# Layer norm of three blocks: the columns of x loaded and normalised on GpSimd, in place of rows normalised and transposed on TensorE

## The chip, the cores and the metric

The kernel runs on one core of one Trainium2 chip. The core has five engines, each with a queue of its own that it works through strictly in order: TensorE (PE in the profile; its weight loads are listed apart as PEld), VectorE (DVE), ScalarE (ACT), GpSimd (POOL) and SyncE (SP, which here only issues DMAs). They wait for each other through semaphores. The metric is the device time of one launch in microseconds (us).

## The reference

One transformer block for S = 2048 tokens of D = 448 values, with 16 heads of 28 and an MLP of 1792 columns, all in float32. A vector `c` gives the scale and shift of both layer norms and the gates:

```python
mod = (silu(c) @ w_mod).reshape(1, 6, 1, 448)
sa, ca, ga, sb, cb, gb = mod[:, 0], ..., mod[:, 5]
h = layernorm(x) * (1 + ca) + sa
x = x + ga * (softmax_attention(h @ wqkv) @ wo)
h = layernorm(x) * (1 + cb) + sb
x = x + gb * (gelu(h @ w1 + b1) @ w2 + b2)
```

The layer norm takes mean and deviation of each token over its 448 values. The change concerns the first layer norm alone, and of it the part for tokens 512 to 2047.

## The kernel before

**Tiling.** The tokens are cut into four blocks of 512 (`NB`), the 448 values into four chunks of 128 (`NC`; the last has 64 values and holds them twice, for a high and a low part). A matmul contracts over the partitions, so the first layer norm's result h has to lie by columns: a chunk is a tile [128 values, 512 tokens]. x lies by rows, [128 tokens, 448 values], four such row tiles to a block. Weights and activations of the dense layers are split into a high part (rounded to the matmul's input type) and a low part (what is left), and a product is three sums of products. Such a product of 448 values takes 11 matmuls (`mm_acc`, L406).

**Stages.** Up to 25 us the kernel loads, computes the modulation and lays block 0 out by columns. Then comes phase 1 (25 to 165 us): the projections to q, k and v, block after block. Phase 2 (165 to 789 us) is the attention in 256 steps, phase 3 (up to the end) the MLP.

**Phase 1.** A loop over the blocks b makes a list of tasks; n counts them. For block 0 they are seven tasks of q and k (n = 0 to 6), four of v (n = 7 to 10), and the first q and k tasks of block 1 (n = 11 and 12); for blocks 1 and 2, five of q and k (n = 0 to 4), four of v (5 to 8), and the next block's first two (9 and 10). A task is 11 matmuls into a PSUM buffer "pa", of which there are two; on PE four or five matmuls for the row maxima of the scores follow it (`emit_task`, L486). DVE reduces each of these (L491); for some, two key chunks are taken in one pass, after a relu by ACT (L499). What maxima are left over when phase 1 ends are done in phase 2, up to three to a step, until step 234.

After a q or k task ACT copies the sum out of PSUM ("full", three buffers, L442), ACT or DVE makes the high part (L445), POOL the low part (L449), and SP stores both (L452); SP also copies the rows that lie over into another place (L388). After a v task ACT copies out of PSUM (L468), which frees the buffer for the next task but one.

**The first layer norm of blocks 1 to 3** is spread over the tasks of the block before. `ln1_stages` has eight stages. Stages 0 to 3 take mean and variance of a row tile (DVE, L209 and L210); the last of them makes variance plus eps (DVE, L214), its power -0.5 (POOL, L216), and minus the mean times that (DVE, then POOL, L277). Stages 4 to 7 write a normalised row tile "xn" (ACT, two instructions, L242 and L243). Then `h_chunk(b + 1, xs, k)` runs at k = n - 6 in block 0 and n - 4 after that: four transposes on PE put a chunk of the four row tiles into one PSUM buffer (L286, called from `transposes`), ACT scales and shifts it by the modulation's columns (L307), ACT makes the high part (L291), POOL the low part (L293, for the last chunk L295). A chunk's transposes stand on PE behind the maxima of task n; its three other instructions stand behind the task's own work on ACT and POOL.

In a task with a `h_chunk`, and in the first four of block 1, `p1_n[1]` is false: the sixth of the PSUM buffers for maxima ("o") is needed for the transposes there, so one maximum fewer can stand beside a pair.

**What sets the order.** Every engine's instructions stand in the order in which this loop emits them. Nothing reorders them on the chip.

Of the kernel before, what the change touches and what calls it, by code (L numbers as in the profile page):

```python
# [13 lines left out]
F32 = mybir.dt.float32  # L14
# [32 lines left out]
def tile_adaln_block(ctx: ExitStack, tc: tile.TileContext, x, wqkv, wo, w1, b1, w2, b2, c, w_mod, out):  # L47
# [90 lines left out]
    for tag, shape, n in (  # L138
        ("mv", [128, 4, 2], 2), ("nm", [128, 4], 1), ("st", [128, 6], 2), ("ve", [128, 4], 2), ("rs", [128, 4], 2),
    ):  # L140
        sbt(tag, shape, bufs=n)
    m32s = [sbt(f"m32_{i}", [128, 32], F32R) for i in range(2)]
    d0 = slot4("d0", [512], F32)
# [120 lines left out]

    def ln1_stages(b):
        mv = []
        mr = []

        def stat(t):
# [3 lines left out]
            if t == 3:  # L273
                nm = sbt("nm", [128, 4])
                dve.tensor_scalar(out=nm, in0=mv[0][:, :, 0], scalar1=-1.0, scalar2=None, op0=ALU.mult)
                rs = ln_rstd(mv[0], 4)
                pool.tensor_tensor(out=nm, in0=nm, in1=rs[0][2], op=ALU.mult)  # L277
                mr.extend([rs[0][2], nm])

        return [lambda xs, t=t: stat(t) for t in range(4)] + [  # L280
            lambda xs, t=t: xs.append(ln1_apply_act(b, t, *mr)) for t in range(4)
        ]
# [16 lines left out]
    def h_chunk(b, xs, k, p=None):  # L299
# [3 lines left out]
        if p is None:  # L303
            p = ps_o()
            transposes(p, xs, k)
# [48 lines left out]
    v_sb = [sb.tile([128, 4, H, 32], F32, tag=f"slot_v{i}", name=f"v{i}", bufs=1) for i in range(4)]  # L354

    def v_init(i):
        pool.memset(v_sb[i][:, :, :, DH : DH + 1], 1.0)
        pool.memset(v_sb[i][:, :, :, DH + 1 : 32], 0.0)
# [164 lines left out]
    for m32 in m32s:  # L523
        pool.memset(f(m32)[:, 16:32], 0.0)

# [280 lines left out]
    for k in range(NC):  # L806
        lo0.append(h_chunk(0, xs0, k, p0[k]))
# [24 lines left out]
    stages = ln1_stages(1)  # L832
    for b in range(NB):
# [8 lines left out]
        if more:  # L842
            stages, later = stages[-4:] if b else stages, ln1_stages(b + 2) if b + 2 < NB else None
            xs_next = []
            tasks += [(b + 1, 0, 0), (b + 1, 1, 0)]
        for n, (tb, kind, g) in enumerate(tasks):
# [10 lines left out]
            p1_n[1] = not (more and (0 <= k < NC)) and not (b == 1 and n < 4)  # L857
# [18 lines left out]
            if more:  # L876
                k = n - (6, 4, 4, 4)[b]

                if b == 0 and n in (0, 1, 3, 4):
                    x = 2 * n if n < 2 else 2 * n - 2  # L880
                    for fn in stages[x : x + 2]:
                        fn(xs_next)
                if b and n < 4:
                    stages[n](xs_next)
# [664 lines left out]
```

## Time and profile before

| | us |
|---|---|
| median of three runs (lowest to highest) | 1091.16 (1090.96 to 1091.35) |
| the profiled execution's own time | 1092.34 |
| its span, from first to last instruction | 1090.6 |
| phase 1, in the span | 25 to 165 |
| PE busy in the span | 1081.5 |
| DVE, ACT, POOL busy in the span | 800.8, 696.7, 231.5 |

The profiled execution took 1.2 us longer than the median, and 1.7 us of it lie outside the span. Stretches are given by the span's clock. A row of the timeline gives the start, the duration of the row in us, the engine, the line of the kernel, the operation, what it writes and reads by the program's names, the shapes, and a count if several alike were joined. A bracket at the end tells how long the engine had been idle, and what it had waited for. SPq rows are DMA issues: the duration is that of the issue on SP, not of the transfer.

### The profile page before, as it was taken

To read this page: it belongs to the slowest core of one execution; us is meant where nothing else is said; L and a number is where in the kernel's file an instruction comes from. 1 tells how busy PE (TensorE), PEld (TensorE's weight loads), DVE (VectorE), ACT (ScalarE), POOL (GpSimd) and SP (SyncE) were. 2 spreads that over 40 slices of the span, in tenths; PEclk is the share of its full clock that TensorE was granted. 3 is DMA by queue.
4 is the path that set the end of the run, shared out by engine and by line. 5 is a ranking of instruction groups with operands and counts; after the bars stand their busy time and mean duration, and the time that the engine had idled before them with its cause. 6 is when DMAs were issued, how large, how long until landed. Compare 5 with 4: busy or idle time off the path is not lost.

```text
span 1090.6 us, 20665 instructions
## 1 busy us (share of the span) xinstructions
PE 1081.5 (99%) x8231; PEld 659.3 (60%) x8231; DVE 800.8 (73%) x1369; ACT 696.7 (64%) x883; POOL 231.5 (21%) x215
## 2 busy tenths in 40 slices
PE   8999999999999999999999999999999999999998
PEld 6766775444444444444444444545488888888887
DVE  6979788999999989988888988584755565464322
ACT  4655657888888888888888888687943321211111
POOL 1543330011011011024231410216114032061000
PEclk9999999999999999999999999999999999999999
DMA  9342262122121201143322423111343301002000
GB/s 304 141 154 74 89 206 86 44 67 57 50 76 61 77 28 58 56 121 86 103 68 78 130 64 95 58 31 60 117 125 96 104 35 47 27 35 73 34 1 34
DMA packets 58870, 88.56 MB, mean 81 GB/s; under 512 B 13807, under 2 KB 25734, under 8 KB 58762
## 3 DMA queue, kind: packets, MB, share of 16 engines
q1 hardware_dynamic: 58290, 86.51, 25.6%
q8 instruction: 64, 1.05, 0.4%
q10 hardware_dynamic: 148, 0.46, 0.1%
q0 software_dynamic: 336, 0.28, 0.1%
q14 instruction: 32, 0.26, 0.1%
HBM read 59.39 MB, written 29.50 MB: 82 GB/s over the span
## 4 chain that ended last, share of the span: by engine, by line
PE 97%; DMA 1%; DVE 1%; ACT 0%; issue 0%; SPq 0%; ACTq 0%
PE s L1392 24%; PE o L1347 23%; PE m L406 17%; PE pa L406 9%; PE m L486 8%; PE s L1484 3%; PE s L1486 3%; PE s L1485 3%; PE s L486 2%; PE t L1485 1%; PE t L1486 1%; PE t L1484 1%; DMA slot_c<-in_w_mod_dram 1%; PE o L286 1%; DVE mxp L491 0%; PE ma L486 0%
## 5 line engine op out<-in xcount | busy, mean ns | idle before, releaser
L491 DVE TENSOR_REDUCE mxp<-m 128x1 f32<-128x512 f32 x553 | 358.3, 686 | 65.5 <-PE m L486 48.9
L1392 PE MATMUL s<-slot_b,slot_a 28*128 28x512 f32 (+1 forms) x3072 | 357.9, 425 | 0.0
L1392 PEld LDWEIGHTS s<-slot_b,slot_a 28*128 28x128 f32 (+1 forms) x3072 | 210.9, 183 | 175.2 <-ACT slot_c L1405 96.4
L486 PE MATMUL m<-kh,qh 28*128 28x512 f32 x606 | 226.0, 469 | 0.8 <-ACT full L780 0.3
L1405 ACT ACTIVATE slot_c<-s 128x1024 f32<-128x1024 f32 x170 | 174.6, 1027 | 51.4 <-PE s L1392 50.4
L1347 PE MATMUL o<-slot_c,v 128*32 128x512 f32 x680 | 178.9, 605 | 0.0
L1440 ACT ACTIVATE full<-m,b_col 128x512 f32<-128x512 f32 x56 | 38.5, 687 | 195.8 <-PE m L406 187.4
L697 DVE TENSOR_REDUCE mxp<-s 128x2 f32<-128x1024 f32 x107 | 131.1, 1226 | 5.1 <-PE s L1392 0.6
L1347 PE MATMUL o<-slot_c1h,v 128*32 128x512 f32 x512 | 134.7, 605 | 0.0
L1347 PE MATMUL o<-slot_c0h,v 128*32 128x512 f32 x508 | 133.6, 605 | 0.0
L1405 ACT ACTIVATE slot_c1h<-s 128x1024 f32<-128x1024 f32 x128 | 130.8, 1022 | 0.0
L1405 ACT ACTIVATE slot_c0h<-s 128x1024 f32<-128x1024 f32 x127 | 130.6, 1028 | 0.0
L1405 ACT ACTIVATE slot_d<-s 128x1024 f32<-128x1024 f32 x86 | 88.3, 1027 | 26.4 <-PE s L1392 26.0
L486 PEld LDWEIGHTS m<-kh,qh 28*128 28x128 f32 x606 | 90.4, 182 | 15.4 <-DVE mxp L491 12.9
L1443 DVE CAST hi<-full 128x512 fp32r<-128x512 f32 x42 | 18.8, 448 | 103.8 <-ACT full L1440 103.7
L1067 POOL TENSOR_TENSOR osb<-osb,osb 128x512 f32<-128x512 f32 x16 | 20.5, 1282 | 344.8 <-DMA osb<-drec 270.9
L1347 PE MATMUL o<-slot_d,v 128*32 128x512 f32 x344 | 90.5, 605 | 0.4 <-ACT osb L1311 0.4
L1444 DVE TENSOR_TENSOR lo<-full,hi 128x512 fp32r<-128x512 f32 x56 | 46.1, 823 | 29.7 <-ACT hi L1443 25.7
L406 PE MATMUL m<-y,slot_a 128*128 128x512 f32 x160 | 60.0, 391 | 0.0
L661 DVE CUSTOM_DVE_ANT_0 slot_d0i<-m,slot_d0i 128x512 f32<-128x512 f32 x55 | 38.1, 692 | 16.5 <-PE m L486 13.8
L1347 PEld LDWEIGHTS o<-slot_c,v 128*32 128x32 f32 x680 | 24.5, 108 | 39.8 <-issue 37.9
L491 DVE TENSOR_REDUCE mxp<-ma 128x1 f32<-128x512 f32 x61 | 39.5, 681 | 11.7 <-PE m L486 6.3
(358 smaller groups left out, 1848.8 us busy)
## 6 DMA issues: line engine op xcount, KB each, us to landing
slot_b<-d SPq DMA_DIRECT2D x32, 256.0 KB
slot_a<-d SPq DMA_DIRECT2D x32, 256.0 KB
d<-lo SPq DMA_DIRECT2D x28, 256.0 KB
d<-hi SPq DMA_DIRECT2D x16, 256.0 KB
osb<-drec SPq DMA_DIRECT2D x15, 256.0 KB
out_dram<-xn SPq DMA_DIRECT2D x16, 224.0 KB
raw<-in_B_w_dram SPq DMA_DIRECT2D x14, 224.0 KB
qh<-d SPq DMA_DIRECT2D x12, 256.0 KB
```

What stands on the lines that cost most here:

```text
L406: pe.matmul(p, a, b, start=(i == 0), stop=(i == len(terms) - 1))
L486: pe.matmul(m, qh_sb[(g, qt)][js, i * 128 : (i + 1) * 128], k[js, :], start=True, stop=True)
L491: dve.tensor_reduce(out=mxp[(g, qt)][:, i, j, cch : cch + 1], in_=m, op=ALU.max, axis=AX.X)
L697: dve.tensor_reduce(out=mxp[(g, qt)][:, i, j : j + 2, cch], in_=t, op=ALU.max, axis=AX.X)
L1347: pe.matmul(o[32 * j : 32 * j + 32, :], v_sb[kt // 4][:, kt % 4, 4 * g + j, :], p[j // 2][:, j % 2, :], start=(kt == 0), stop=(kt == NKT - 1),
L1392: pe.matmul(s2[:, jj, :], ks[rows_, kp, kc], qs[rows_, qp, :], start=(term == 0), stop=(term == 2))
L1405: act.activation(pt[hf], s2, AF.Exp, scale=SCALE)
L1440: act.activation(gf, p, AF.Gelu_apprx_tanh, bias=b1_col[:, i : i + 1])
L1444: dve.tensor_tensor(out=glo, in0=gf, in1=f(ghi), op=ALU.subtract)
L1484: pe.matmul(pp, ghi[:, ts], w_hi, start=(m == 0), stop=False)
L1485: pe.matmul(pp, ghi[:, ts], w_lo, start=False, stop=False)
L1486: pe.matmul(pp, glo[:, ts], w_hi, start=False, stop=(m == NFT - 1))
```

## The change

The host passes one more input, `x_cols`: blocks 1 to 3 of x, transposed, so that a chunk [128 values, 512 tokens] is one DMA. The chunks of a block go into the four buffers "xn" that held the normalised row tiles.

The statistics still come from the row tiles on DVE. Mean and deviation now go into columns of one tile [128, 32]; DVE transposes it in squares of 32 (L295), four DMAs of SP write the rows to memory off the core (L298), and two more read them back, broadcast to 128 partitions (L300): a tile with the mean of each token along the row, and one with the deviation's inverse. This is the stage `rows_out`. The stage `apply(k)` then subtracts the first and multiplies by the second, in place, on POOL (L304, L305). ACT's scale and shift reads that chunk from SBUF in place of PSUM (L329, was L307); there are no transposes.

For block 1, task n = 0 and 1 of block 0 hold the statistics, n = 2 `rows_out`, n = 3 nothing, n = 4 to 7 the four `apply`. For blocks 2 and 3 the statistics stand at n = 6 to 9 of the block two before, `rows_out` at n = 10, and `apply` at n = 0 to 3 of the block before. `h_chunk` stays at its tasks. `p1_n[1]` is always true. The instruction counts of the two programs differ as follows: 48 transposes fewer on PE, 24 row normalisations fewer on ACT, 24 operations of 128x512 more on POOL (and three small ones fewer, two memsets more), 33 DMAs more on SP (15 loads of columns, 12 writes and 6 reads of rows). The buffer for DMA descriptors is set to 8192 bytes. Ten of the maxima's matmuls move from phase 2 (steps 230 to 234) to phase 1; steps 231 to 234 hold none any more.

```diff
+    def load_x_cols(b, k):
+        t = xn_t()
+        x_cols[(b, k)] = t
+        if k < 3:
+            sp.dma_start(t, x_t[b - 1, 128 * k : 128 * k + 128, :])
+        else:
+            for h in range(2):
+                sp.dma_start(t[64 * h : 64 * h + 64], x_t[b - 1, 384:D, :])
...
             if t == 3:
-                nm = sbt("nm", [128, 4])
-                dve.tensor_scalar(out=nm, in0=mv[0][:, :, 0], scalar1=-1.0, ...)
-                rs = ln_rstd(mv[0], 4)
-                pool.tensor_tensor(out=nm, in0=nm, in1=rs[0][2], op=ALU.mult)
-                mr.extend([rs[0][2], nm])
+                st = st32[b % 2]
+                dve.tensor_copy(st[:, 0:4], mv[0][:, :, 0])
+                ve = sbt("ve", [128, 4], bufs=2)
+                dve.tensor_scalar(out=ve, in0=mv[0][:, :, 1], scalar1=EPS, ..., op0=ALU.add)
+                pool.tensor_tensor(out=st[:, 4:8], in0=ve, in1=neg_half, op=ALU.pow)
-            lambda xs, t=t: xs.append(ln1_apply_act(b, t, *mr)) for t in range(4)
+        def rows_out():
+            r = sbt("r32", [128, 32], bufs=2)
+            dve.transpose(r, st32[b % 2])
+            dst = ln_dr[b % 2].rearrange("c (t p) -> (c t) p", p=128)
+            for i in range(4):
+                sp.dma_start(dst[:, 32 * i : 32 * i + 32], r[32 * i : 32 * i + 8, :])
+            for c_ in range(2):
+                sp.dma_start(mr_row(b, c_), ln_dr[b % 2, c_][None].broadcast_to([128, 512]))
+
+        def apply(k):
+            y = x_cols[(b, k)]
+            pool.tensor_tensor(out=y, in0=y, in1=mr_row(b, 0), op=ALU.subtract)
+            pool.tensor_tensor(out=y, in0=y, in1=mr_row(b, 1), op=ALU.mult)
...
-        if p is None:
-            p = ps_o()
-            transposes(p, xs, k)
...
-            p1_n[1] = not (more and (0 <= k < NC)) and not (b == 1 and n < 4)
+            p1_n[1] = True
...
-                if b == 0 and n in (0, 1, 3, 4):
-                    x = 2 * n if n < 2 else 2 * n - 2
-                    for fn in stages[x : x + 2]:
-                        fn(xs_next)
+                if b == 0 and n < 8:
+                    for fn in (stages[0:2], stages[2:4], stages[4:5], (), *([fn] for fn in stages[5:]))[n]:
+                        fn()
                 if b and n < 4:
-                    stages[n](xs_next)
+                    stages[n]()
                 if 0 <= k < NC:
-                    post.append(h_chunk(b + 1, xs_next, k))
+                    post.append(h_chunk(b + 1, k, x_cols[(b + 1, k)]))
-                if later and 7 <= n < 11:
-                    later[n - 7](None)
+                if later:
+                    if 6 <= n < 11:
+                        later[n - 6]()
+                    if 2 <= k < NC + 2:
+                        load_x_cols(b + 2, k - 2)
...
+    x_cols = np.asarray(A_x)[0].reshape(NB, 128, 4, D).transpose(0, 3, 2, 1).reshape(NB, D, 512)[1:]
```

Two places show how the order on the queues moves. The first is POOL in block 0's tasks, from the low part of task 3 ("raw") to the chunks of block 1's h ("slot_c"; the last row is the last chunk's low part). Before:

```order
L449 TENSOR_TENSOR lo_398<-full_397,raw_396 128x512
L449 TENSOR_TENSOR lo_441<-full_440,hi_439 128x512
L449 TENSOR_TENSOR lo_483<-full_482,hi_481 128x512
L357 MEMSET v_239 128x64
L358 MEMSET v_239 128x64x3
L449 TENSOR_TENSOR lo_519<-full_518,hi_517 128x512
L293 TENSOR_TENSOR slot_c_119_523<-full_530,slot_c_117_521 128x512
L293 TENSOR_TENSOR slot_c_119_523<-full_572,slot_c_117_521 128x512
L293 TENSOR_TENSOR slot_c1h_524<-full_612,slot_c0h_522 128x512
L295 TENSOR_TENSOR slot_c0h_522<-full_649,slot_c0h_522 64x512
```

With the change, from the same low part on (xn_339, xn_341, xn_343 and xn_345 are the chunks 0 to 3 of block 1, slot_v_90 the two broadcast rows):

```order
L481 TENSOR_TENSOR lo_418<-full_417,raw_416 128x512
L304 TENSOR_TENSOR xn_339<-xn_339,slot_v_90_401 128x512
L305 TENSOR_TENSOR xn_339<-xn_339,slot_v_90_401 128x512
L481 TENSOR_TENSOR lo_455<-full_454,hi_453 128x512
L304 TENSOR_TENSOR xn_341<-xn_341,slot_v_90_401 128x512
L305 TENSOR_TENSOR xn_341<-xn_341,slot_v_90_401 128x512
L481 TENSOR_TENSOR lo_493<-full_492,hi_491 128x512
L304 TENSOR_TENSOR xn_343<-xn_343,slot_v_90_401 128x512
L305 TENSOR_TENSOR xn_343<-xn_343,slot_v_90_401 128x512
L389 MEMSET v_243 128x64
L390 MEMSET v_243 128x64x3
L481 TENSOR_TENSOR lo_531<-full_530,hi_529 128x512
```

Behind these rows stand, one after the other, the low part of chunk 0, the pair on xn_345, the low parts of chunks 1 and 2, the power of block 2's statistics (L291), and the low part of chunk 3. So four pairs of operations on whole chunks now stand between the low parts on the same queue, and each pair reads the two broadcast rows.

The second place is SP in the same tasks. Before, from the store of task 1's low part to that of task 3's high part "raw" ("kh" is task 2's high part, "d" the memory off the core):

```order
L452 DMA d_248<-lo_351 128x512
L388 DMA d_254<-d_243 4x4x512
L388 DMA d_258<-d_247 4x4x512
L452 DMA d_251<-kh_81_372 128x512
L452 DMA d_255<-lo_374 128x512
L388 DMA d_254<-d_244 4x4x512
L388 DMA d_258<-d_248 4x4x512
L452 DMA d_252<-raw_396 128x512
```

With the change:

```order
L484 DMA d_251<-lo_365 128x512
L420 DMA d_257<-d_246 4x4x512
L420 DMA d_261<-d_250 4x4x512
L484 DMA d_254<-kh_86_383 128x512
L484 DMA d_258<-lo_385 128x512
L420 DMA d_257<-d_247 4x4x512
L420 DMA d_261<-d_251 4x4x512
L298 DMA ln_dr<-r_89_395 8x32 x4
L300 DMA slot_v_90_401<-ln_dr 128x512 x2
L484 DMA d_255<-raw_416 128x512
```

The six new DMAs stand behind the stores of the tasks before and ahead of the store of task 3's high part.

37 lines of the change are left out of this document (25 added, 12 removed).

## The prediction

> **What bounds the kernel now.** I read the page's busy shares first, then the chain of waits, then the busy times of phase 1 block by block.
>
> ```profile
> PE 1081.5 (99%) x8231; PEld 659.3 (60%) x8231; DVE 800.8 (73%) x1369; ACT 696.7 (64%) x883; POOL 231.5 (21%) x215
> PE 97%; DMA 1%; DVE 1%; ACT 0%; issue 0%; SPq 0%; ACTq 0%
> ```
>
> ```profile
> core 0: us, PE busy (x) PEld busy (x) DVE busy (x) ACT busy (x) POOL busy (x), PEclk, DMA share, GB/s
> 25.00:56.00 31.00, 31.00 (x161) 23.37 (x160) 29.91 (x64) 17.55 (x31) 17.92 (x18) 1.00 0.40 149
> 56.00:98.00 42.00, 41.62 (x204) 28.10 (x203) 32.95 (x67) 24.25 (x45) 16.38 (x16) 1.00 0.32 107
> 98.00:131.00 33.00, 32.83 (x169) 22.83 (x169) 26.90 (x61) 24.14 (x46) 14.42 (x15) 1.00 0.32 118
> ```
>
> PE is busy for 99% of the span and makes 97% of the chain. In the three stretches that hold the tasks of blocks 0, 1 and 2 it never stands still for more than 0.4 us in all. So any time in which PE has to wait is added to the end, and any matmul taken away comes off, if nothing else holds PE. POOL's 21% over the span misleads: in the first stretch it is busy for 17.92 of 31 us, and that is where the change puts its first eight large operations.
>
> **Part 1: the transposes go.**
>
> ```profile
> L286 PE MATMUL o<-ident,xn x48: 272/273/329, 37.1 to 126.1; 128*128 128x128 f32 x48
> 37.10 0.66 PE L286 MATMUL o<-ident,xn 128*128 128x128 f32 x4
> 37.51 1.87 PE L406 MATMUL pa<-slot_e,slot_b 128*128 128x448 f32 x8
> ```
>
> These 48 are the transposes of blocks 1 to 3, in twelve groups of four. A group holds PE from 37.10 to the next start at 37.51, 0.41 us; twelve make 4.9 us, or 1.65 per block. This is the most that PE can win in phase 1. The blocks decide how much of it is kept.
>
> **Part 2: block 1's rows go off the core and back.** The four writes and two broadcasts stand on SP behind task 2's stores, which wait for POOL's low part, and behind two copies of rows.
>
> ```profile
> 34.34 1.22 SPq L388 DMA_DIRECT2D d<-d  x2
> 35.61 0.45 SPq L452 DMA_DIRECT2D d<-raw  x1
> ...
> 219.02 0.33 SPq L1060 DMA_DIRECT2D drec<-den  x1
> 220.47 0.54 SPq L1062 DMA_DIRECT2D osb<-drec  x1
> ...
> 574.03 0.53 SPq L781 DMA_DIRECT2D drow<-full  x1
> 575.74 0.32 SPq L784 DMA_DIRECT2D row_b2g<-drow  x1
> ```
>
> ```profile
> 29.57 0.52 POOL L277 TENSOR_TENSOR nm<-nm,rs 128x4 f32<-128x4 f32 x1
> ...
> 32.73 1.28 POOL L449 TENSOR_TENSOR lo<-full,raw 128x512 fp32r<-128x512 f32 x1
> ```
>
> The copies end at 35.56. POOL's small product of 29.57 goes, so its queue and what follows run 0.5 earlier: SP comes to the new DMAs at 35.1. Four writes at 0.33 (row 219.02) put the last issue at 36.1. The program already has such a trip, a write followed by a broadcast that waits for it: issue to issue it takes 1.71 (574.03 to 575.74) or 1.45 (219.02 to 220.47). With 1.71 the first broadcast is issued at 37.8. For its landing the nearest rows are the four broadcasts to 128 partitions issued from 575.74 on:
>
> ```profile
> 577.00:578.00 1.00, 1.00 (x16) 0.18 (x12) 1.00 (x2) 0.81 (x1) 0.92 (x2) 1.00 0.83 210
> 578.00:579.00 1.00, 1.00 (x15) 0.59 (x11) 0.77 (x3) 1.00 (x2) 0.39 (x1) 1.00 1.00 289
> ```
>
> Data moves from about 577.0, 1.2 us after the first issue, at up to 289 GB/s. Two broadcasts of 262 KB are 524 KB, 1.8 us. So both rows lie in SBUF at X = 37.8 + 1.2 + 1.8 = **40.8**. From below: 1.45 for the trip and SP's copies 0.4 shorter give 39.7. From above there is the program's broadcast from DRAM of the same size:
>
> ```profile
> 721.64 0.54 SPq L1062 DMA_DIRECT2D osb<-drec  x1
> 726.62 1.29 POOL L1067 TENSOR_TENSOR osb<-osb,osb 128x512 f32<-128x512 f32 x1 [22.12 <-DMA osb<-drec]
> ```
>
> Its reader starts 5.0 after the issue. With 0.61 for each write (the copies of 34.34) this gives X = 35.1 + 1.8 + 1.7 + 0.4 + 5.0 = 44.0. I take 40.8, because the rows of 575.74 have the change's form (one row, 128 partitions) and osb<-drec has four rows to 32 partitions each. [...]
>
> **Part 3: POOL's queue from X on.** POOL finished task 3's low part at 33.5 (34.0 less 0.5) and then stands still until X, and with it everything behind in its queue: the low parts of tasks 4, 5 and 6, and all four chunks of block 1. From X it works without a gap:
>
> ```profile
> 745.13 1.14 POOL L1129 TENSOR_TENSOR xn<-xn,row_cb 128x448 f32<-128x448 f32 x1
> 746.35 1.15 POOL L1130 TENSOR_TENSOR xn<-xn,row_sb 128x448 f32<-128x448 f32 x1
> 42.15 2.53 POOL L293 TENSOR_TENSOR slot_c<-full,slot_c 128x512 fp32r<-128x512 f32 x2
> 39.54 0.31 POOL L358 MEMSET v<- 128x192 f32 x1
> 102.23 1.01 POOL L216 TENSOR_TENSOR rs<-ve,cst 128x4 f32<-128x4 f32 x1 [1.74 <-DVE ve L214]
> ```
>
> An operation of 512 columns takes 1.28, or 1.26 from start to start where two stand in a row (2.53 for two). Where the second needs the first, 1.22 instead of 1.14 (rows 745.13 and 746.35): 0.08 more. A pair of `apply` therefore takes 1.36 + 1.25 = 2.6. Four pairs 10.4, six low parts 7.6, two memsets 0.4 (the kind of 39.54), the power 1.0, the last low part 1.3: 20.7. ACT is held along with it. Its scale and shift of chunk k waits for pair k, and the v tasks' copies out of PSUM stand behind that in ACT's order; with two PSUM buffers PE stops at the third v task. What PE could still do stands behind that matmul.
>
> ```profile
> 52.38 0.61 PE L406 MATMUL pa<-slot_c0h,slot_a 128*128 128x512 f32 x2
> 52.92 0.50 PE L486 MATMUL m<-raw,osb 28*128 28x512 f32 x2
> ```
>
> Block 1's first q task needs the last low part. Before it ended at 52.92, its last two matmuls (52.38) taking 0.55. Now it ends at 40.8 + 20.7 + 0.55 = 62.05, **9.1 later** (8.0 with X = 39.7, 12.3 with 44.0). The block's 1.65 from the transposes is within this: PE waits anyway.
>
> **Part 4: block 1's tasks.**
>
> ```profile
> 60.24 1.89 DVE L491 TENSOR_REDUCE mxp<-m 128x1 f32<-128x512 f32 x3 [3.90 <-PE ma L486]
> 62.05 0.68 DVE L491 TENSOR_REDUCE mxp<-ma 128x1 f32<-128x512 f32 x1
> 60.90 1.29 POOL L449 TENSOR_TENSOR lo<-full,osb 128x512 fp32r<-128x512 f32 x1 [0.81 <-ACT osb L445]
> ```
>
> PE is relieved of 1.65 us, but with the sixth PSUM buffer allowed, about seven more maxima are done here. On PE they run beside others; on DVE each takes 0.60 (62.05 less 60.24, by three): 4.2 us. DVE's idle time in 56 to 98 is 42 - 32.95 = 9.05, of which 3.90 stand before the row at 60.24; 5.15 remain, and 3.5 once PE is 1.65 shorter. The 4.2 do not quite fit: between -1.65 and +0.7, I take -0.4.
>
> **Part 5: block 2's tasks.** Block 3's rows leave in the last task of block 1, behind that task's maxima on DVE, so they land some 9 us after block 2 begins by the same trip, and four pairs stand between the low parts (10.4 us of POOL in a stretch in which POOL had 33 - 14.42 = 18.6 idle). By the queue the first chunk could be ready some 2 to 3 us later than before, with relus and copies of ACT behind it; buffers take part of that. Between -1.65 and +1.3, I take -0.2.
>
> **Part 6: phase 2.** Steps 231 to 234 lose their maxima. These are the first exponentials of steps 231, 232 and 234 to 237:
>
> ```profile
> 728.32 1.02 ACT L1405 ACTIVATE slot_d<-s 128x1024 f32<-128x1024 f32 x1 [0.34 <-PE s L1392]
> 730.65 1.04 ACT L1405 ACTIVATE slot_c<-s 128x1024 f32<-128x1024 f32 x1
> ...
> 739.77 1.02 ACT L1405 ACTIVATE slot_d<-s 128x1024 f32<-128x1024 f32 x1 [0.38 <-PE s L1392]
> 744.33 1.02 ACT L1405 ACTIVATE slot_c<-s 128x1024 f32<-128x1024 f32 x1 [0.37 <-PE s L1392]
> 748.72 1.02 ACT L1405 ACTIVATE slot_c<-s 128x1024 f32<-128x1024 f32 x1 [0.32 <-PE s L1392]
> 750.68 1.02 ACT L1405 ACTIVATE slot_d<-s 128x1024 f32<-128x1024 f32 x1
> ```
>
> Step 234 with maxima took 4.56, step 235 without 4.39: 0.17 each for 232 to 234. Step 231 took 2.33, step 236 without maxima 1.96, of which I take 0.3. Together **-0.8** (0 to -1.2). The other edits lie beside PE: ACT has 24 operations fewer and is no bound, and the loads of columns are issued by 31 and needed at X.
>
> **The sum:** 9.1 - 0.4 - 0.2 - 0.8 = **+7.7**. The profiled span goes from 1090.6 to 1098.3, its own time from 1092.34 to 1100.0. The median shown is 1.2 below that execution, so it goes from 1091.16 to **1098.9**.
>
> **Rivals.**
>
> *PE takes the saving.* PE is the bound and loses 4.9 in phase 1 and 0.8 in phase 2: 1085.5. For it speaks the 99%; against it, that even with rows that came without delay POOL's queue would end block 1's chunks too late, as the next rival shows. It holds only if POOL's operations take about half of row 745.13.
>
> *The rows' trip is hidden, POOL alone decides.* X = 33.5, the q task ends at 33.5 + 21.25 = 54.75, 1.8 later; with the other terms +0.4, so 1091.6. Against it: SP's rows 34.34 and 35.61 show when SP is free.
>
> *The rows land as slowly as osb<-drec, in block 2 too.* 12.3 - 0.4 + 1.3 - 0.8 = +12.4, so 1103.6. Other stores are in flight at 37 to 40, as beside osb<-drec.
>
> *POOL and DVE hinder each other.*
>
> ```profile
> 33.27 1.23 DVE L204 TENSOR_TENSOR slot_e<-slot_v,slot_e 128x448 fp32r<-128x448 f32 x1
> 37.15 0.61 DVE L204 TENSOR_TENSOR slot_e<-slot_v,slot_e 128x448 fp32r<-128x448 f32 x1
> ```
>
> With POOL's operation of 32.73 beside it, DVE's subtraction took twice as long. If the maxima suffered so in block 1, where POOL gets eight operations more (8 x 1.28 = 10.2), DVE would lose 5.1 with no idle time left: +12.8, 1104.0. Against it: the three reductions from 60.24 took 0.60 each with POOL's operation of 60.90 beside the middle one. [...]
>
> **How the numbers follow.** Chances: the forecast 0.65; slow rows 0.15; hindrance 0.04; trip hidden 0.06; PE's saving 0.10. Within 0.2% (2.2 us), about what this measurement can tell from no change, lies only the trip hidden, so same 0.06; faster is PE's saving, 0.10; slower the rest, 0.84. The range goes from 1093.0 (between trip hidden and the forecast's low end, 1091.16 + 8.0 - 1.65 - 1.65 - 1.2 = 1094.7) to 1105.5 (12.3 + 0.7 + 1.3 = +14.3).
>
> **What would show it.** In the profile after: POOL idle for some 7 us ahead of the first subtraction at L304, released by a DMA from ln_dr, at about 40.8; PE idle in 42 to 62 for some 10 us altogether, at the v tasks and the q task after them; that q task's end near 62; from there on the two kernels within 1 us of a constant distance up to step 230; steps 231 to 234 shorter by 0.17 to 0.3. I am wrong in the sign if L304 starts before 36 or a pair takes less than 1.5; wrong in size if the distance still grows or shrinks by over 2 us in 62 to 131.

## The result, and the profile after

The changed kernel takes 1122.46 us (median of 5 runs, 1121.15 to 1124.67), the kernel before 1091.16: a ratio of 1.0289 (95% interval 1.0278 to 1.03), 31 us slower. The sign was forecast, the size was not: 7.7 us were expected. The profiled execution, the slowest of the five, took 1124.67 us with a span of 1122.9, 32.3 more than before.

Two rows of the changed kernel's page (before, PE is busy for 99% and POOL for 21% of the span, and PE makes 97% of the chain):

```profile
PE 1095.8 (98%) x8183; PEld 663.4 (59%) x8183; DVE 802.3 (71%) x1374; ACT 688.1 (61%) x863; POOL 260.8 (23%) x238
PE 88%; DVE 3%; POOL 1%; DMA 0%; issue 0%; ACT 0%; SPq 0%; DVEq 0%; POOLq 0%
```

PE has 48 matmuls fewer and is busy for 14.3 us more. Not all of the 32 us is standing still; matmuls also became slower. The clock column of the windows shows it. These are stretches of the changed kernel, with the same columns as in the prediction:

```profile
core 0: us, PE busy (x) PEld busy (x) DVE busy (x) ACT busy (x) POOL busy (x), PEclk, DMA share, GB/s
44.00:48.00 4.00, 0.12 (x1) 0.00 (x0) 3.86 (x9) 1.63 (x3) 3.92 (x4) 1.00 0.23 89
48.00:52.00 4.00, 3.72 (x11) 3.31 (x11) 0.29 (x2) 2.06 (x4) 3.92 (x4) 0.57 0.40 149
62.00:69.00 7.00, 6.06 (x16) 4.11 (x17) 2.48 (x4) 1.20 (x2) 2.16 (x2) 0.51 0.49 152
96.00:100.00 4.00, 4.00 (x16) 2.60 (x16) 1.73 (x6) 0.67 (x2) 1.22 (x1) 0.57 0.35 126
106.00:110.00 4.00, 4.00 (x12) 3.16 (x11) 2.70 (x7) 0.06 (x1) 1.28 (x1) 0.57 0.21 26
137.00:144.00 7.00, 0.56 (x1) 0.28 (x1) 1.92 (x6) 1.13 (x3) 6.84 (x7) 0.52 0.45 165
144.00:148.00 4.00, 4.00 (x12) 3.28 (x11) 1.81 (x5) 1.69 (x3) 4.00 (x6) 0.56 0.40 149
161.00:165.00 4.00, 4.00 (x16) 2.63 (x14) 0.65 (x4) 0.00 (x0) 0.00 (x0) 0.57 0.01 4
```

Six times after 48 us the granted clock falls, within a us, from 1.00 to 0.50, for about 3.4 us or two or three times that. In the kernel before it never does (1.00 in all four stretches of phase 1). PE's busy time by one minus the clock, summed over slices of 1 us, is the time lost at half clock: 4.7 us in block 0's tasks, 3.4 in block 1's, 3.7 in block 2's. It is an upper bound of what it cost in the end, since slow work beside something longer costs nothing.

To place the rest, I compare the copies out of PSUM on ACT, one per task, with those of the kernel before. The first copy alone shifts by -1.9 to +1.2 us between executions, before any edit acts; it is taken off. A block's row ends with the copy of the next block's first task. The steps after phase 1 are compared by their exponentials.

| us later than before | forecast | measured | lost at half clock |
|---|---|---|---|
| block 0's tasks | +9.1 | +14.2 | 4.7 |
| block 1's tasks | -0.4 | +6.6 | 3.4 |
| block 2's tasks | -0.2 | +10.0 | 3.7 |
| block 3's tasks and the steps up to 227 | 0 | +1.2 | 0 |
| steps 228 to 231 | (in the next) | +1.6 | 0 |
| steps 232 to 235 | -0.8 | -0.8 | 0 |

Wherever the sixth maximum is always allowed, the copy that ends block 2's row comes 0.9 us earlier against the kernel before than the copies on both sides of it. There 0.9 us of the row below belong to block 2.

What PE waited for in phase 1 (the six largest waits of PE between 25 and 196 us: total, number, longest; before, the whole list is one wait of 0.3):

```profile
PE o L518 <- DVE mxp L535: 6.8, 1, 6.8
PE pa L438 <- ACT v L500: 4.8, 2, 4.2
PE pa L438 <- POOL slot_c0h L320: 1.8, 1, 1.8
PE pa L438 <- POOL slot_c L318: 1.2, 1, 1.2
PE m L518 <- ACT slot_d L531: 0.8, 1, 0.8
PE pa L438 <- POOL slot_c1h L318: 0.7, 1, 0.7
```

The second row is the third v task and the POOL rows are block 1's first q task: the stalls of Part 3, in their places. The first row, the longest, stands in block 2's tasks and was not foreseen. Its other end is a wait of DVE, released by POOL:

```profile
142.08 0.69 DVE L535 CUSTOM_DVE_ANT_0 slot_d0h<-m,slot_d0h 128x512 f32<-128x512 f32 x1 [8.72 <-POOL mxp L515]
```

```profile
130.45 1.30 POOL L304 TENSOR_TENSOR xn<-xn,slot_v 128x512 f32<-128x512 f32 x1 [9.63 <-DMA slot_v<-ln_dr]
...
140.69 1.26 POOL L481 TENSOR_TENSOR lo<-full,hi 128x512 fp32r<-128x512 f32 x1
141.89 0.15 POOL L515 MEMSET mxp<- 128x64 f32 x1
142.00 1.27 POOL L304 TENSOR_TENSOR xn<-xn,slot_v 128x512 f32<-128x512 f32 x1
```

DVE stood for 8.7 us for a memset of 0.15 us: the tile that collects the maxima of a new group is cleared on POOL (L515), and that instruction stood in POOL's queue behind three pairs of `apply`, which waited for block 3's rows (the first at 130.45). DVE then freed no buffer for maxima, and PE stood behind DVE.

### The profile page after: what moved, and what is told of

The parts are those of the page before. It is cut to its first block, busy times and chain, and to the rows that moved or that the text cites. A ratio compares the mean times of both kernels' runs of the same rounds, so it can differ in the third digit from the quotient of the medians.

```text
span 1122.9 us, 20621 instructions
## 1 busy us (share of the span) xinstructions
PE 1095.8 (98%) x8183; PEld 663.4 (59%) x8183; DVE 802.3 (71%) x1374; ACT 688.1 (61%) x863; POOL 260.8 (23%) x238
## 4 chain that ended last, share of the span: by engine, by line
PE 88%; DVE 3%; POOL 1%; DMA 0%; issue 0%; ACT 0%; SPq 0%; DVEq 0%; POOLq 0%
PE s L1429 23%; PE o L1384 23%; PE m L438 16%; PE m L518 7%; PE pa L438 5%; PE s L1521 3%; PE s L1523 3%; PE s L1522 3%; DVE mxp L523 3%; PE s L518 2%; PE t L1523 1%; PE t L1522 1%; PE t L1521 1%; POOL xn L305 0%; DMA slot_v<-ln_dr 0%
## 5 line engine op out<-in xcount | busy, mean ns | idle before, releaser
L523 DVE TENSOR_REDUCE mxp<-m 128x1 f32<-128x512 f32 x546 | 353.3, 686 | 70.7 <-PE m L518 50.5
L518 PE MATMUL m<-kh,qh 28*128 28x512 f32 x594 | 221.3, 471 | 1.8 <-ACT slot_d L531 0.8
L731 DVE TENSOR_REDUCE mxp<-s 128x2 f32<-128x1024 f32 x105 | 128.7, 1226 | 4.7 <-PE s L1429 0.3
L518 PEld LDWEIGHTS m<-kh,qh 28*128 28x128 f32 x594 | 88.0, 182 | 18.9 <-DVE mxp L523 15.0
L518 PE MATMUL s<-kh,qh 28*128 28x512 f32 x212 | 47.5, 437 | 0.8 <-DVE mxp L523 0.8
```

The lines of the kernel that those rows point to most:

```text
L518: pe.matmul(m, qh_sb[(g, qt)][js, i * 128 : (i + 1) * 128], k[js, :], start=True, stop=True)
L523: dve.tensor_reduce(out=mxp[(g, qt)][:, i, j, cch : cch + 1], in_=m, op=ALU.max, axis=AX.X)
L731: dve.tensor_reduce(out=mxp[(g, qt)][:, i, j : j + 2, cch], in_=t, op=ALU.max, axis=AX.X)
```

## The experiments

What block 0's tasks and the others lose or win is this shift against the kernel before, where no other run is named. Most kernels here ran once, with the profiler; they are compared by the shift and by their own time. The kernel before took 1090.6 to 1091.0 us beside them.

### What block 2's stall was: the memset, and the rule for the sixth maximum

The memset moved to VectorE, in the changed kernel:

```diff
-                (pool if (g, qt) in paired else dve).memset(mxp[(g, qt)], -3.0e38)
+                dve.memset(mxp[(g, qt)], -3.0e38)
```

> The change, with the memsets of the maxima's tiles on VectorE in place of GpSimd. Theory (the 8 us in block 2's tasks are the wait of VectorE for a memset of 0.14 us that stands in GpSimd's queue behind block 3's applies): that wait and the 6.8 us of TensorE behind it go, and a part of the half-clock stretch after it; 1112 to 1116 us. Rival (the low parts that stand behind the same applies hold ScalarE's three buffers anyway, and TensorE waits for ScalarE in its place): within 3 us of the change's 1122.5.

It took 1121.68 us, in the rival's range. The waits of 8.7 and 6.8 us are gone, and block 2's tasks lose 5.0 us in place of 10.0. But three of these five came back: up to step 227 this run lost 4.3 in place of 1.2. At the start of phase 2 PE waits for a DMA (first row), and right behind that it works for a stretch at half clock, which loses 1.7 us (second row, the columns of the windows):

```profile
189.84 0.50 PE L1429 MATMUL s<-slot_b,slot_a 29*128 29x512 f32 x2 [1.11 <-DMA slot_b<-full]
191.90:195.31 3.41, 3.41 (x10) 3.06 (x11) 0.99 (x2) 0.92 (x2) 0.00 (x0) 0.50 0.87 282
```

The theory was right on the wait. What its end is worth in the total, one execution does not show: whether the edit brought the DMA's wait about stays open.

The rule for the sixth maximum as before, all else as in the change:

```diff
-            p1_n[1] = True
+            p1_n[1] = not (more and (0 <= k < NC)) and not (b == 1 and n < 4)
```

> The change with the rule for the sixth maximum as it was before, so that maxima stand where they stood. Theory (block 1's tasks lose their 6.7 us because seven maxima more make TensorE wait for VectorE, and the thin stretches then let the clock fall to half): block 1's tasks lose under 3 us, 1115 to 1119 us. Rival (they lose it by GpSimd's late low parts): within 2 us of the change's 1122.5.

1111.74 us, better than the theory: block 1's tasks lose nothing (-0.1 in place of +6.6), no half-clock stretch lies in them, and the stall at step 230 is gone too. One line of the change costs about 11 us.

Both edits at once:

> The change with the rule for the sixth maximum as before and the memsets of the maxima's tiles on VectorE, both at once; all three blocks by columns, order otherwise as in the change. Theory (three causes that add up: the sixth maximum, the memset behind the applies, block 1's late rows and GpSimd chain): block 1's tasks lose nothing, block 2's tasks lose 1 to 3 us in place of 8, and what is left is block 0's 11 to 13 us; 1104 to 1108 us. Rival (in block 2 the low parts behind the applies hold TensorE as long as the memset did): 1109 to 1112 us, as with the rule alone (1111.7).

1110.88 us, in the rival's range. Block 0's tasks lose 14.0 here (12.6 with the rule alone: the order is the same there, and the four runs with it gave 12.1 to 14.2). Block 2's lose 5.4, in place of 8.0 with the rule alone: less, but not the 1 to 3 of the theory. PE waits only 2.5 us there now, for relus of ACT, and then runs at half clock for ten:

```profile
136.00:147.00 11.00, 10.77 (x34) 7.24 (x35) 6.67 (x14) 6.56 (x11) 7.77 (x9) 0.53 0.30 110
```

10.77 us of work at 0.53 are 5.0 us lost. The wait was shortened, and the clock took most of the gain.

### What PE could have saved

The kernel before, with the transposes left out, so that ACT takes the row tile where a chunk belongs (h has the wrong layout):

```diff
-            p = ps_o()
-            transposes(p, xs, k)
+            p = xs[k]
```

> The kernel before with the 48 transposes left out: ScalarE scales and shifts the row tiles as if they were chunks (so h is not the layer norm of the right shape); rows are normalised as before, no applies, no rows' trip, no loads of columns, the maxima stand where they stood. Theory (in the tasks of blocks 0 and 1 VectorE's reductions set the pace, and TensorE can keep its 1.65 us only in block 2): 1088.5 to 1090.5 us. Rival (TensorE is the bound in all three): 1085.5 to 1087 us.

1088.3 us. Block 0's tasks win 0.6 us, block 1's 0.8, block 2's 1.2: 2.6 of the 4.9. The time is 0.2 under the theory's range and 1.3 over the rival's. Why block 0 keeps so little is seen on PE. First the kernel before, then the run without transposes, both times the maxima behind the third v task and what follows them:

```profile
46.47 0.50 PE L486 MATMUL ma<-raw,osb 28*128 28x512 f32 x2
46.48 0.50 PE L486 MATMUL m<-raw,osb 28*128 28x512 f32 x2
46.91 0.66 PE L286 MATMUL o<-ident,xn 128*128 128x128 f32 x4
```

```profile
43.83 0.49 PE L485 MATMUL ma<-raw,osb 28*128 28x512 f32 x2
43.84 0.91 PE L485 MATMUL m<-raw,osb 28*128 28x512 f32 x2
44.68 1.92 PE L405 MATMUL pa<-slot_e,slot_b 128*128 128x448 f32 x8
```

The four maxima take 0.44 us before, and 0.85 where no transposes follow: just the 0.41 that were left out. Behind the other three of these tasks the difference is 0.35, 0 and 0.21, so 1.0 of the block's 1.65 us is lost in this way. The last maximum starts late because it needs a PSUM buffer that DVE has to free: here it begins at 44.25, 0.05 us after a reduction ends (44.20). This wait reads as busy PE: the row of 43.84 counts 0.91 us for two matmuls, the row of 46.47 counts 0.50.

The same with the sixth maximum always allowed:

```diff
-            p1_n[1] = not (more and (0 <= k < NC)) and not (b == 1 and n < 4)
+            p1_n[1] = True
```

> As the run without transposes, and the sixth maximum always allowed, as in the change. Theory (the ten maxima that move into phase 1 overload VectorE in block 1's tasks, whatever GpSimd does): 4 to 7 us lost in block 1's tasks, 1 to 2 at step 230, 0.8 won in steps 232 to 234; 1093 to 1098 us. Rival (the maxima only hurt beside GpSimd's work): within 1 us of the run without transposes.

1096.89 us, 8.6 more than without it, 1.4 of this by a later first copy. Against the run without transposes block 1's tasks lose 3.9, block 2's win 0.8 (all of it by the early copy named above), block 3's and the steps up to 227 lose 2.0, steps 228 to 231 2.9, and steps 232 to 235 win 0.8. There is no half-clock stretch in phase 1 of this run, and none of GpSimd's new work. So the seven maxima more (4.2 us of DVE) cost block 1 nearly their full time, and DVE stays behind: at step 230, the last one with maxima, PE waits for them. Behind that wait the clock falls for 3.4 us, which loses 1.7 of the 2.9:

```profile
728.72 0.40 PE L485 MATMUL s<-kh,qh 28*128 28x512 f32 x1
729.90 0.49 PE L485 MATMUL s<-kh,qh 28*128 28x512 f32 x1 [0.78 <-DVE mxp L490]
730.94:734.36 3.42, 3.42 (x24) 1.07 (x20) 3.25 (x11) 1.38 (x2) 0.00 (x0) 0.50 0.02 4
```

The changed kernel has the same wait at step 230 (0.79 us), without a slow stretch behind it.

### GpSimd's operations and the rows' trip

The 24 operations left out, so that h comes from columns that are not normalised:

```diff
         def apply(k):
             y = x_cols[(b, k)]
-            pool.tensor_tensor(out=y, in0=y, in1=mr_row(b, 0), op=ALU.subtract)
-            pool.tensor_tensor(out=y, in0=y, in1=mr_row(b, 1), op=ALU.mult)
```

> The change with the 24 operations on GpSimd left out (h comes from columns that are not normalised); loads, statistics and the trip of the rows stay. Theory (nothing but the applies waits for the rows, and the loads hide): TensorE keeps the 4.9 us of the transposes, less what the ten maxima more cost in block 1's tasks (0 to 5 us): 1086 to 1092 us. Rival (the extra loads and DMAs of SP, or the maxima moved to phase 1, cost by themselves): over 1094 us.

1102.33 us: the rival. The maxima make most of it (block 1's tasks +5.4, steps 228 to 231 +1.6), as its second half has it. But block 0's tasks also lose 2.8 us with no `apply` in them. POOL shows why:

```profile
44.76 1.29 POOL L479 TENSOR_TENSOR lo<-full,hi 128x512 fp32r<-128x512 f32 x1 [5.17 <-DMA d<-lo]
```

Its low part waits for a buffer whose store stands on SP behind the rows' trip: SP waits there between the writes and the broadcasts, with the stores behind. This cost of the trip the prediction did not have.

The opposite, the trip left out: the applies read one constant row of ones (so h is not the layer norm).

```diff
         def rows_out():
-            r = sbt("r32", [128, 32], bufs=2)
...
-                sp.dma_start(mr_row(b, c_), ln_dr[b % 2, c_][None].broadcast_to([128, 512]))
+            if not one_row:
+                one_row.append(sbt("one_row", [128, 512]))
+                dve.memset(one_row[0], 1.0)
```

> The change, where the rows of mean and deviation don't leave the core: the writes and broadcasts are left out, and the applies read one constant row of ones that is there early (so h is not the layer norm). Theory (the lateness of the rows starts all three of GpSimd's jams, its operations themselves fit): the first subtraction starts at about 33.5 us, block 1's first q task ends 2 to 4 us later than in the kernel before in place of 11, block 2's wait of 7 us is gone; 1097 to 1103 us. Rival (GpSimd's 24 operations are what costs, whenever they start): that q task still ends over 8 us later, 1110 us or more.

1107.65 us, between theory and rival. Block 0's tasks lose 4.6, a little more than the theory's 2 to 4, and block 2's nothing (-0.2), as it has it; block 1's lose 6.8. That this is the sixth maximum, the old rule beside it shows:

> As the run in which the rows don't leave the core (constant rows of ones, so h is not the layer norm), with the rule for the sixth maximum as before; memsets on GpSimd as in the change. Theory (without the trip only GpSimd's own chain in block 0's tasks costs, 4 to 5.5 us; the memset of 0.14 us hurts only while GpSimd stands still for rows): block 1's and block 2's tasks lose nothing, 1093.5 to 1096.5 us. Rival (the applies also hold up blocks 1 and 2): 1098 us or more.

1096.39 us: block 0's tasks +4.7, block 1's -0.1, block 2's -1.0, with the memsets still on POOL. So GpSimd's operations by themselves cost 4.7 us in block 0's tasks and nothing in the other two blocks (0.8 us more are lost up to step 227).

### When the rows land

The six DMAs of the trip issued by ScalarE, in the changed kernel:

```diff
-                sp.dma_start(dst[:, 32 * i : 32 * i + 32], r[32 * i : 32 * i + 8, :])
+                act.dma_start(dst[:, 32 * i : 32 * i + 32], r[32 * i : 32 * i + 8, :])
...
-                sp.dma_start(mr_row(b, c_), ln_dr[b % 2, c_][None].broadcast_to([128, 512]))
+                act.dma_start(mr_row(b, c_), ln_dr[b % 2, c_][None].broadcast_to([128, 512]))
```

> The change, with the six DMAs of each rows_out issued by ScalarE in place of SyncE, so that they don't stand behind the stores of task 2 (in the change they wait there from 28.9 us, when the rows are transposed, to 35.2). Theory (the place on SyncE's queue is 6 of the trip's 14 us): the first subtraction at 35 to 38 us in place of 42.5, block 0's loss falls from 13.4 to 6 to 9 us, block 2's stall by 2 to 4; 1108 to 1117 us. Rival (the trip off the core and back is the long part wherever it is issued): the first subtraction stays after 40 us, 1119 us or more.

1128.97 us, worse than the change and in neither range. The first subtraction did start at 36.38, as expected, but block 0's tasks still lost 11.1. ACT now stood for the trip itself: its copy out of PSUM of 32.86 had been held for 7.9 us, and in block 2 PE's wait behind the memset grew from 6.8 to 13.1. A queue that waits must be one with nothing behind it.

Block 1's rows sent out right behind their statistics, on SP, ahead of the stores of task 1 and 2 (old rule, memsets on DVE):

```diff
-                    for fn in (stages[0:2], stages[2:4], stages[4:5], (), *([fn] for fn in stages[5:]))[n]:
+                    for fn in (stages[0:2], stages[2:5], (), (), *([fn] for fn in stages[5:]))[n]:
```

> As the run with the old rule and VectorE's memsets, and block 1's rows are sent out one task earlier, right behind their statistics, so that their six DMAs stand on SyncE ahead of the stores of tasks 1 and 2. Theory (block 0's loss follows the time at which the rows land, one to one): the first subtraction at 35 to 37 us in place of 40 to 42, and 3 to 5 us less than the run without this edit. Rival (the stores that now wait behind the trip hold the low parts' buffers, and GpSimd's own chain is the longer part): within 2 us of it.

1102.18 us, 8.7 less than without the edit. The first subtraction starts at 35.17 in place of 42.23, 7.1 earlier, and block 0's tasks lose 6.6 in place of 14.0, 7.4 less. That this looks like one to one is luck: 2.7 of the 7.4 are a stretch at half clock behind POOL's chain, which is gone: where PE waited 5.0 us for ACT's copies of v and 3.8 for POOL's low parts without the edit, it now waits 1.3, for a low part. The other 4.7 are what was expected. They are less than the 7.1 mainly because POOL's chain, from the first subtraction to the last low part, takes 22.3 us here in place of 20.4.

Block 3's rows early too (statistics in tasks 3 to 6, `rows_out` in task 7 of block 1):

> As the run with block 1's rows sent early (old rule, memsets on VectorE), and block 3's statistics in tasks 3 to 6 and its rows_out in task 7 of block 1, three tasks earlier. Theory (late rows make block 2's loss; where they are in time the four applies fit beside the tasks): block 2's tasks lose nothing or win up to 1.7 us in place of losing 4.6, no half-clock stretch there, 1095.5 to 1098.5 us. Rival (the four applies between the low parts hold the buffers whenever the rows come): block 2's tasks still lose 3 us or more, 1100.5 us or more.

1097.73 us. Block 2's tasks win 1.6 us in place of losing 4.7: with the rows in time four applies fit beside them. That is about the block's 1.65, but the run without transposes, which has no applies at all, wins 1.2 there; so a part may be time that block 1's tasks had lost just before. These now lose 2.2, with one half-clock stretch (1.7).

### The clock

26 matmuls more, into a PSUM buffer that nobody reads, where PE stood in block 0's tasks of the changed kernel: 14 ahead of the third v task, 4, 2 and 6 ahead of the low parts in block 1's first q task.

```diff
+    def warm_fill(count, a, b):
+        w = ps_o()
+        for _ in range(count):
+            pe.matmul(w[:, : b.shape[-1]], a, b, start=True, stop=True)
...
+            if b == 0 and n in (9, 11):
+                fill.append({0: 14} if n == 9 else {7: 4, 8: 2, 9: 6})
```

> The change, with 26 matmuls more on TensorE whose result nobody reads: 14 where it waits for ScalarE ahead of the third v task of block 0, 4, 2 and 6 where it waits for GpSimd's low parts in block 1's first q task. They lie in time in which TensorE stood still for 4.2 and 3.8 us. Theory (the clock falls to 0.50 because TensorE stood still, and that makes 3 to 5 of block 0's 13.4 us): the half-clock stretches at 48 to 52 and 62 to 69 us are gone, the copy of block 1's first k task comes 8 to 9.5 us later than in the kernel before (11.0 to 13.4 in the three runs that had both stalls), 1116 to 1120 us, faster with more work. Rival (the fall has another cause, or the stall is what costs): the copy comes 11 us later or more, 1121 us or more.

```profile
62.00:69.00 7.00, 6.80 (x31) 5.22 (x32) 2.48 (x4) 2.73 (x5) 2.93 (x4) 1.00 0.56 174
102.00:113.00 11.00, 10.89 (x30) 7.64 (x30) 7.36 (x16) 1.90 (x4) 1.27 (x1) 0.53 0.16 20
```

The half-clock stretches in block 0 are gone (first row; 0.51 in the change), so standing still was their cause. The copy came 9.9 us later than before rather than 11.0 to 13.4 (with the shift of the first copy taken off, 10.9 rather than 12.1 to 14.2). It is a little less of a gain than expected: a part of the slow time lay beside POOL's chain, which sets the end. The total was 1123.71, no gain. In block 1's tasks the clock fell for 3.4 us and then for ten (second row), where it had fallen twice for 3.4, and these tasks lost 9.6 in place of 6.6, which took back what was won. Ahead of that stretch PE stands nowhere for over half a us. What these falls have in common is shown in the last section.

### Versions meant to keep the saving

Block 3 alone by columns, blocks 1 and 2 as before, the old rule, the memsets on DVE, and block 3's rows in time. First with the statistics in tasks 3 to 6 of block 1:

> A version meant to keep what TensorE can keep: blocks 1 and 2 by rows and transposes as in the kernel before, only block 3 by columns, its statistics in tasks 3 to 6 and its rows_out in task 7 of block 1, the memsets on VectorE, the rule for the sixth maximum as before. Theory (block 2's tasks are the only ones in which TensorE is the bound, and there the rows are in time): 0.8 to 1.6 us less than the kernel before, 1089.5 to 1090.4 us. Rival (four applies between the low parts delay block 2's tasks all the same): 1 to 4 us more than before.

1091.16 us (11 runs) against 1090.95: a ratio of 1.0001 (0.9992 to 1.001), no difference. Block 2's tasks win their 1.6 us, but block 1's lose 3.0 in the profiled execution, 1.7 of it by one half-clock stretch, behind statistics that DVE now does in its fullest tasks. Block 2 by columns as well:

> As the version with block 3 by columns, and block 2 by columns too (statistics in tasks 5 to 8, rows_out in task 9 of block 0, loads in tasks 10 and 11). Theory (VectorE paces block 1's tasks, so that little more is won there, 0 to 0.8 us): 1088.7 to 1090.4 us. Rival (block 2's rows come too late for block 1's first tasks, or GpSimd's four pairs hold them): over 1092 us.

1091.65 us, ratio 1.0008 (0.9999 to 1.0018): the same. Then block 3 alone with its statistics late again, and its applies two each in tasks 3 and 4:

> Block 3 alone by columns as in the earlier version, but its statistics at tasks 6 to 9 and rows_out at task 10 of block 1, as in the change, and its applies at tasks 3 and 4 of block 2 (two each) in place of 0 to 3, so that no low part waits for the rows. Theory (statistics in block 1's tasks 3 to 6 cost VectorE what TensorE then lacks; behind them block 2's saving is kept): block 1's tasks within 0.3 us of before, block 2's 1.0 to 1.7 less; 0.8 to 1.6 us less than the kernel before. Rival (the columns' loads or rows disturb block 1, or the bunched applies block 2): within 0.5 us of the kernel before or slower.

1097.73 us, ratio 1.0054 (1.0041 to 1.0068): the rival. Block 1's tasks lose only 0.7, so the early statistics had been the cause there. But block 2's lose 6.5, 4.8 of it in a half-clock stretch of 10.2 us. The copy of the block's first v task waited 5.9 us on ACT, since v's tile shares its buffer with the rows and its memset stands behind four applies:

```profile
ACT v L528 <- POOL xn L330: 5.9, 1, 5.9
```

At last the applies one each in tasks 3 to 6, and the rows in another buffer:

> Block 3 alone by columns, statistics at tasks 6 to 9 and rows_out at task 10 of block 1 as in the change, its applies one each at tasks 3 to 6 of block 2, and the rows in the buffer of block 3's v in place of block 2's, so that v's memset doesn't wait for the last apply. Theory (with statistics late and applies spread nothing on GpSimd's queue is late): block 1's tasks lose 0 to 0.7 us, block 2's win 1.0 to 1.7; 0.3 to 1.7 us less than the kernel before. Rival (an apply ahead of a chunk's low part is on the path of block 2's v tasks): block 2's tasks no shorter than before, the same or more than the kernel before.

1092.95 us (11 runs), ratio 1.0022 (1.001 to 1.0033), the rival: block 2's tasks are as long as before, in a profiled execution that was the fastest of the eleven (1091.11). No complete version tried here beats the kernel before.

## Why the prediction was right and wrong

**What bounds the kernel.** This is the step that failed first. I read PE's 99% as PE being the only bound and the DVE column of the same row, 29.91 of 31 us, not at all. In block 0 DVE was as full as PE: the transposes stood in time in which PE, as the run without them shows, waits for buffers that DVE frees. In block 1 (32.95 of 42) 0.8 of the 1.65 was kept. Hence Part 1's 4.9 us could not be had (2.6 in the run without transposes), and the rival that PE takes the saving was wrong for this reason too, not only for POOL's.

**Part 2, the trip**, held in its path and was short in its size. The first subtraction was forecast for 40.8 and came at 42.46, 41.13, 40.44 and 42.23 in the four kernels that have the change's order in block 0. But these executions started 0.8 to 1.5 us earlier than the profile before; by its clock they came at 41.9 to 43.3, late by 1.1 to 2.5. In the changed kernel SP came to the writes at 35.21 (35.1 forecast), issued the broadcasts at 38.40 (37.8), and the rows took 4.1 from there (3.0). The lower bound, 39.7, is a slip: its two terms give 40.1.

```profile
35.21 1.48 SPq L298 DMA_DIRECT2D ln_dr<-r  x4
38.40 0.82 SPq L300 DMA_DIRECT2D slot_v<-ln_dr  x2
```

```profile
42.46 1.28 POOL L304 TENSOR_TENSOR xn<-xn,slot_v 128x512 f32<-128x512 f32 x1 [8.94 <-issue]
43.81 1.27 POOL L305 TENSOR_TENSOR xn<-xn,slot_v 128x512 f32<-128x512 f32 x1
...
61.62 1.26 POOL L320 TENSOR_TENSOR slot_c0h<-full,slot_c0h 64x512 fp32r<-64x512 f32 x1
```

Of the rivals on the trip, hidden it was not. And the 4.1 us of the rows lie midway between the 3.0 of the forecast and the 5.0 of osb<-drec: that rival was half right in block 0.

**Part 3, POOL's chain**, held: 20.4 us from the first subtraction to the end of the last low part (20.7 forecast), with a pair of 2.57. Block 0's 14.2 us are, to within 0.4, the 9.1 of the forecast, 2.5 by which the rows came later, and 3.0 at half clock. What was missing is the clock: behind its stalls PE worked for 3.4 and 6 us at half speed. The first of these two stretches lies beside POOL's chain and shows no price; the second lies behind the chain's end and loses the 3.0. The run with 26 matmuls more, without slow stretches in block 0, lost 10.9 there. The prediction let the clock stay at 1.00 because it did so in every stretch of the profile; but in those PE never stood for more than 0.3 us at a time, so the profile did not show the clock behind a stall. The changed kernel does: the stretch at 48 us, 3.4 us at 0.50, came behind a stall of 4.2; that at 62 began in the last of three waits of 0.7 to 1.8 with single matmuls between them; and those in block 1 had no wait of over 0.2 in the 3.4 us ahead of them.

**Part 4** was right that 4.2 us of reductions meet 3.5 us of idle time, and wrong to take that idle time as usable. It lies in pieces, where the next maximum is not there yet (in 56 to 98 us before, five waits for PE, 8.9 us in all), and the maxima cost 3.9 us in the run that has them alone. That is the term that was mis-sized, -0.4 for +3.2, and the clock adds 3.4.

**Part 5** is the largest miss: -0.2 became +10.0. I listed the low parts as what stands behind the applies on POOL. The memset of the maxima's tile stood there too, and DVE waits for it. The rows also came later than forecast: the first apply started at 130.45, 12.5 us after the block's first task began on PE, in place of some 9, and behind a standing POOL. With the rows in time, or without the trip, and the old rule, the block's tasks win 1.0 to 1.6 us.

**Part 6** came out at its size where it was worked out from rows: 0.84 for steps 232 to 235. But work that leaves steps 231 to 234 must be done before, and steps 228 to 231 paid 1.6 for it, at the wait of step 230.

**The rival of hindrance** between POOL and DVE did not show in the maxima: in phase 1 of the changed kernel the 42 reductions that lie beside POOL's operations of 512 columns took 0.68 us on average, as did the 40 with none beside them.

## What to carry to other kernels

A busy share of 99% on one engine does not say that the others have room: look at every engine in the same stretch, and take away the work that you mean to save before you pay for its replacement. When a new wait enters a queue, write down every instruction behind it, the smallest too, and who waits for each; here DVE stood for 8.7 us for a memset of 0.15. And a stall of the matrix engine can have a second price behind it, its slow clock: in the changed kernel 3.4 us at 0.50 right behind 4.2 us of standing.

## What the runs showed of the hardware

- In the changed kernel the granted clock moved in steps. It fell to exactly 0.50 at 48.5, 62.2, 96.3, 106.5, 137.3 and 161.2 us. These times lie 4, 10, 3, 9 and 7 steps of 3.41 us apart, and the clock stayed low for one, two, one, one, three and one step. At 137.3 PE had stood for only 0.6 of the 6.8 us. PE's busy share did not tell when it fell: here are the steps just ahead of the two falls in block 1's tasks, and the second step behind the later fall.

```profile
92.89:96.31 3.42, 3.16 (x12) 1.86 (x12) 3.42 (x6) 2.35 (x4) 1.48 (x2) 1.00 0.42 138
103.13:106.55 3.42, 2.92 (x8) 1.37 (x8) 3.42 (x7) 2.35 (x4) 0.36 (x1) 1.00 0.22 33
109.96:113.37 3.41, 3.41 (x18) 2.28 (x17) 2.75 (x6) 1.02 (x2) 0.00 (x0) 1.00 0.21 26
```

  PE is busy for 92% and 85% of the first two, but with 12 and 8 matmuls in place of 18. In the second, five of them are maxima, which use 28 of the 128 rows and start some 0.6 us apart, as fast as DVE's reductions free buffers:

```profile
103.15 0.50 PE L518 MATMUL m<-raw,qh 28*128 28x512 f32 x1
103.84 0.50 PE L518 MATMUL m<-raw,osb 28*128 28x512 f32 x1 [0.20 <-DVE mxp L523]
104.44 1.09 PE L518 MATMUL ma<-raw,osb 28*128 28x512 f32 x2
105.64 0.50 PE L518 MATMUL m<-kh,qh 28*128 28x512 f32 x1
```

  Count each matmul that starts in a step by the share of 128 rows and of 512 columns that it uses. In phase 1 the middle one of the steps that kept the clock has 11.8 by this count in the kernel before, and 11.2 in the changed one. In the traces of all eighteen kernels, from 30 us on 5544 such steps at full clock, the clock fell behind all 24 steps with less than 5, behind 12 of 23 with 5 to 6.5, and behind 1 of 5497 with more; in the changed kernel alone, behind 4 of 4, 2 of 3 and none of 302. The bounds are drawn from these counts alone. So in the changed kernel the sixth maximum made PE's work thin enough, 6.3 and 2.8 in the two steps above, for the clock to fall without a long stall; with the rule for it as before no half-clock stretch lay in block 1's tasks.

- In the changed kernel the write of the rows off the core and their broadcast back took 7.2 us from the first issue to the first use (35.21 to 42.46), of which SP alone was held for 4.0, with the stores of other tasks behind it.
- One subtraction of DVE on SBUF took far longer beside POOL's operations on whole chunks: 0.61 us at 27.99 in the changed kernel, 1.56 at 28.78, while POOL's low parts of 28.58 and 29.82 ran. That every such operation does so was not shown: in the kernel before, a cast of DVE took 0.42 at 28.54 with none of them beside it, and 0.42 at 29.94 beside the low part that began at 30.04.

```profile
27.99 0.61 DVE L205 TENSOR_TENSOR slot_e<-slot_v,slot_e 128x448 fp32r<-128x448 f32 x1
28.64 0.21 DVE L295 STREAM_TRANSPOSE r<-st 128x32 f32<-128x32 f32 x1
28.78 1.56 DVE L205 TENSOR_TENSOR slot_e<-slot_v,slot_e 128x448 fp32r<-128x448 f32 x1
```
